# Scores and value products of a full attention as two streams over seven shared exponential buffers

## The chip, the cores and the metric

The kernel runs on one core of a Trainium2 chip. The metric is the device time of one execution in microseconds (us); lower is better. TensorE is called PE in the profile, VectorE DVE, ScalarE ACT, GpSimd POOL, and SyncE, which here only issues DMAs, SP.

## The reference

Four residual layers run in turn on x of 2048 rows by 512 columns: A, B, A, B, each behind a layer norm.

```python
# A: 32 query heads of 16, one shared key and value head
p = softmax(einsum("bhqd,bkd->bhqk", q, k) * 16 ** -0.5)        # 32 x 2048 x 2048
o = einsum("bhqk,bkd->bhqd", p, v)
x = x + o.reshape(S, 512) @ wo
# B: four segments of 512 rows, causal inside a segment, 32 heads of 16,
#    and a memory M, z that earlier segments leave behind
p = softmax(einsum(qs, ks) * 16 ** -0.5 + causal_mask)
a_mem = (phi(qs) @ M) / (phi(qs) @ z + 1e-6)
o = sigmoid(beta) * a_mem + (1 - sigmoid(beta)) * (p @ vs)
M, z = M + phi(ks).T @ vs, z + sum(phi(ks))
x = x + o @ wo
```

Everything is float32 outside; inside, projections are split into two parts each and scores into bf16 parts.

## The kernel before

**The full attention (A).** Its work is cut into units: one block `b` of 512 query rows, one group `n` of four heads, key tiles `k0` to `k1` of 128 keys. For each key tile there are two *scores*, each eight matmuls into a pair of PSUM banks (`bank<-qa,kst`, four column tiles of the array times two heads), and behind each score one *exponential* on ACT that reads the pair and writes 128 x 1024 numbers to SBUF (`pa<-bank`, line 640). Then comes one *value product* for the key tile: four float32 matmuls in the four column tiles (`bank<-pa,va`; each shows as two in the trace), which add to the one bank `pva`. The last product of a unit is followed by a transpose on DVE (line 669), and the first product of the next waits for it. There are 1024 key tiles: 2048 scores and exponentials and 1024 products.

**The windowed attention (B) and the rest.** A `side` is everything else that one block needs: the output projection of A (`out_norm`), the norm, the projections (lines 378, whole array, twelve matmuls into one bank), B's row maxima (`bank<-kb,qb`, with DVE line 838 behind them), B's scores (`bank<-qb,kb`), exponentials (`pb<-bank`, line 873) and products (`bank<-pb,vb`), the memory, and B's output projection. Projections and transposes use the whole array; scores, row maxima and products of both attentions use it as four column tiles.

**What sets the order.** The program is one stream per engine, in order. `a_units` is a Python generator that yields a time function before each step; `weave` runs it against the generator of a `side`. `weave` keeps a planned clock per engine (`clk`), asks both generators when their next step can start, adds a charge for a change of tiling (`2 * DRAIN`, 190 ns) and a small one for the one that is ahead (`LAG`), and writes the step with the lower sum. When the side is done, `finish` writes what is left of A in this phase. There are eight phases: phase 0 weaves A's first block with the preparation (norm, keys, queries), phases 1 to 7 weave one block of A with the side of the block before. After phase 7 the last side runs alone.

**Buffers.** `rings["sc"]` is the ring of PSUM pairs for scores: three pairs while A runs alone, two when A and B are woven, and then both attentions' scores take from the same ring. A pair is free again when its exponential has run. Exponentials of A rotate over four SBUF buffers (`pa`), those of B over three (`pb`). One bank (`r`) serves the projections of a woven side and one (`m`) its row maxima.

In `a_units` the order within A is fixed: score, score, then the product of the key tile before (`pend`). In `b_attend` it is: all scores of a key tile, then the product of the tile before.

Of the kernel before, what the change touches and what calls it, by code (L numbers as in the profile page):

```python
# [29 lines left out]
F32 = mybir.dt.float32  # L30
# [7 lines left out]
P = 128  # L38
# [3 lines left out]
GUARD_MAX = 160.0  # L42
KA = 5
# [28 lines left out]
def net_kernel(ctx, tc, x_in, a_wq, a_wk, a_wv, a_wo, b_wq, b_wk, b_wv, b_wo, b_beta, cst, out):  # L72
# [115 lines left out]
    xl = st([P, 4, 512], F32R, "xl")  # L188
    bank = ps_1.tile([P, 8, 512], F32, tag="bank", name="bank")
# [112 lines left out]
    class Need:  # L302


        def __init__(self, at, form):
            self.at, self.form_ = at, form
# [34 lines left out]
    def weave(za, ta, gb, tb):  # L341

        zb = [gb, next(gb)]
        da = db = 0.0
        while zb[1] is not None:
            now, ra, rb = clk["pe"], za[1]() if za[1] else 1e18, zb[1]()
            lag = (da / ta - db / tb) * (ta + tb) / 2

            def score(z, r, ahead):
                return max(now, r) + (2 * DRAIN if form_of(z[1]) != tiling[0] else 0.0) + LAG * ahead  # L350

            use = za if za[1] and score(za, ra, lag) <= score(zb, rb, -lag) else zb
# [252 lines left out]
    def a_units(units):  # L605

        def gate(f, n, k1):
            return 0.0 if f <= phase[0] or (f == phase[0] + 1 and (n == 0 or k1 < 16)) else 1e18  # L610

        def load(ui):
            L, _, b, n, _, _ = units[ui]
            return a_load(L, b, n) if L["qr"][b][n // 2] < 1e17 else None

        pend = None
        nxt = load(0)
        for ui, (L, f, b, n, k0, k1) in enumerate(units):
            if pend is not None and (gate(f, n, k1) or nxt is None):
                yield Need(lambda: max(pend[-1], pva_free[0] if pend[1] else 0.0), "cols")  # L620
                a_pv(*pend)
                pend = None
            if nxt is None:
                yield lambda: L["qr"][b][n // 2]
                nxt = load(ui)
            q, need = nxt
            if L["exact"]:
                need = yield from a_exact_guard(L, q, need)
            rows = 98 if L["exact"] else 97
            for kt in range(k0, k1):  # L630
                pe_, te = [], []
                for u in range(2):
                    yield Need(lambda: max(need, rings["sc"].ready(), L["kr"][kt // 4], gate(f, n, k1)), "cols")
                    ring = rings["sc"]
                    k, sc = ring.take()
                    for i in range(2):
                        by_columns(i == 0, sc[:, i, :], L["kst"][0:rows, kt * P:(kt + 1) * P],
                                   q[0:rows, 2 * u + i, :], start=True, stop=True)
                    x = tmp(4, [P, 2, 512], F32, "pa")
                    A.activation(x, sc, AF.Exp, scale=0.25)  # L640
                    ring.free[k] = on("act", pe(432, "cols"), 904)
                    pe_.append(x)
                    te.append(ring.free[k] + HOP)
                if kt == k0 + 1 or (kt == k0 and k1 - k0 == 1):
                    nxt = load(ui + 1) if ui + 1 < len(units) else None
                if kt == max(k0, k1 - 3) and (b, n) in L["part"]:
                    L["old"] = tmp(2, [P, 16, 32], F32, "xn")
                    nc.sync.dma_start(L["old"], L["part"].pop((b, n)))
                if pend is not None:
                    yield Need(lambda: max(pend[-1], pva_free[0] if pend[1] else 0.0), "cols")  # L650
                    a_pv(*pend)
                pend = (L, kt == k0, kt, pe_, (f, b, n, k0, k1), kt == k1 - 1, max(te))
        yield Need(lambda: max(pend[-1], pva_free[0] if pend[1] else 0.0), "cols")
        a_pv(*pend)
# [3 lines left out]
    def a_pv(L, first, kt, x, unit, last, _):  # L658
# [3 lines left out]
        for j in (2, 3, 0, 1):  # L662
            together(j == 2, pva[32 * j:32 * j + 17, :], lhsT=L["va"][:, kt, 0:17], rhs=x[j // 2][:, j % 2, :],
                     start=first, stop=last)
        e = pe(848, "cols")
        if not last:
            return
# [182 lines left out]
    def b_attend(b, n, r, last):  # L850
# [3 lines left out]
        for kt in range(4):  # L854
            nq = 512 - kt * P
            es, loc = [], ([(0, 0), (1, 0)] if kt < 2 else [(0, 0), (0, nq)])
            for s_ in range(1 if kt >= 2 else 2):
                yield Need(lambda: max(gr[n], rings["sc"].ready()), "cols")
# [13 lines left out]
                e = tmp(3, [P, 2, 512], F32, "pb")  # L872
                A.activation(e[:, :, 0:w], sc[:, :, 0:w], AF.Exp, scale=0.25)  # L873
# [40 lines left out]
    def b_pv(t, p, kt, nq, es, loc, _):  # L914
        for j in (2, 3, 0, 1):
# [3 lines left out]
                     rhs=es[s_][:, i, o_:o_ + nq], start=kt == 0, stop=kt == 3)  # L919
        pe(nq * 4 / 2.4, "cols")  # L920

# [188 lines left out]
```

## Time and profile before

| | |
|---|---|
| time, median of 3 runs | 3312.0 us (3307.43 to 3313.17) |
| the profiled execution: its time, its span | 3313.73 us, 3311.9 us |
| PE busy | 3161.7 us (95%) |
| ACT busy | 2378.2 us (72%) |
| DVE busy | 1643.2 us (50%) |
| POOL busy | 404.4 us (12%) |
| mean share of the 16 DMA engines | 18.0% for the queues of SP, 6.9% for those of POOL |
| granted TensorE clock | 0.992 of full speed |

How to read it: a matmul's row has a start and a drawn length, but matmuls are pipelined: the next group can start while the last one is still drawn. So the distance between two starts is what a group costs, and a short wait of PE can lie hidden under the drawn length. "L81" is the first matmul of a group in column tiles, "L84" the others, "L378" a projection. "Idle before" is the time in which an engine had nothing drawn, with what ended it.

### The profile page before, as it was taken

Reading aid. Unit: us, or ns where it says so; the run is one execution under the profiler, and the core shown is the slowest. Engines: PE = TensorE matmul, PEld = TensorE weight load, DVE = VectorE, ACT = ScalarE, POOL = GpSimd, SP = SyncE. Lnnn points to the kernel's source line nnn. Section 1 sums busy time; section 2 is a strip of 40 time slices with the busy share of each in tenths; the row PEclk is TensorE's granted clock in tenths of the full one; section 3 lists DMA queues with packets and bytes.
Section 4 is the critical chain, followed back from the end, with each engine's and each line's share of the span. In section 5 each row is a group of like instructions: output and inputs, shape, how many; then the busy total and the mean of one; then the engine's idle time right before and its main releaser. Section 6 shows DMA issues by size and latency. Waiting matters only on the chain.

```text
span 3311.9 us, 99350 instructions
## 1 busy us (share of the span) xinstructions
PE 3161.7 (95%) x43490; PEld 1550.1 (47%) x43490; DVE 1643.2 (50%) x4487; ACT 2378.2 (72%) x2575; POOL 404.4 (12%) x564
## 2 busy tenths in 40 slices
PE   7999999999999999999999999999999999999987
PEld 4533445444444444444444444454444444444554
DVE  7711355354654545644455453565445534454465
ACT  3599677866778667786677868677678886778533
POOL 2100111021100211101210020100110003100011
PEclk9999999999999999999999999999999999999999
DMA  4411222122220222202322142421221204421351
GB/s 132 129 42 31 61 82 61 32 76 88 68 68 17 75 77 72 66 27 65 100 84 81 45 121 84 117 65 50 87 84 47 65 25 139 126 62 41 104 147 50
DMA packets 188853, 247.56 MB, mean 75 GB/s; under 512 B 26904, under 2 KB 147576, under 8 KB 188408
## 3 DMA queue, kind: packets, MB, share of 16 engines
q1 hardware_dynamic: 169272, 176.08, 18.0%
q0 software_dynamic: 19136, 65.02, 6.9%
q8 instruction: 343, 5.62, 0.7%
q14 instruction: 102, 0.84, 0.1%
HBM read 168.41 MB, written 72.61 MB: 73 GB/s over the span
## 4 chain that ended last, share of the span: by engine, by line
PE 56%; ACT 17%; issue 11%; DVE 9%; DMA 4%; POOL 3%; SPq 0%; ACTq 0%; DVEq 0%; POOLq 0%
PE bank L81 30%; ACT pa L640 14%; PE bank L84 13%; PE bank L378 12%; ACT pb L873 3%; DMA wst<-in_B_wk_dram 2%; POOL w L134 1%; DVE w L222 1%; DVE m L813 1%; PE bank L438 1%; DVE mo L838 1%; DVE qf L456 1%; DVE rest L465 1%; POOL parts L134 1%; DVE parts L467 1%
## 5 line engine op out<-in xcount | busy, mean ns | idle before, releaser
L640 ACT ACTIVATE pa<-bank 128x1024 f32<-128x1024 f32 x2048 | 1985.2, 1030 | 536.9 <-PE bank L84 525.4
L84 PE MATMUL bank<-qa,kst 97*32 97x512 bf16 x14336 | 1175.9, 382 | 0.4 <-DVE qmx L508 0.4
L81 PE MATMUL bank<-pa,va 128*17 128x512 f32 x2048 | 1053.8, 595 | 13.3 <-DVE t L669 8.7
L84 PE MATMUL bank<-pa,va 128*17 128x512 f32 x6144 | 1063.4, 596 | 0.0
L81 PE MATMUL bank<-qa,kst 97*32 97x512 bf16 x2048 | 781.1, 381 | 40.7 <-ACT pa L640 18.0
L838 DVE CUSTOM_DVE_ANT_0 mo<-bank,maskq 128x256 bf16<-128x256 f32 (+3 forms) x896 | 436.4, 487 | 482.4 <-PE bank L84 471.6
L84 PEld LDWEIGHTS <-kst 97*32 97x32 bf16 x14336 | 360.2, 96 | 391.0 <-issue 327.1
L873 ACT ACTIVATE pb<-bank 128x1024 f32<-128x1024 f32 (+2 forms) x384 | 329.5, 881 | 179.5 <-PE bank L84 177.3
L81 PEld LDWEIGHTS <-kst 97*32 97x32 bf16 x2048 | 194.3, 95 | 379.2 <-issue 299.2
L378 PE MATMUL bank<-xh,w 128*128 128x512 f32 x832 | 292.2, 413 | 5.8 <-DVE qmx L508 3.0
L81 PEld LDWEIGHTS bank<-pa,va 128*17 128x17 f32 x2048 | 184.1, 97 | 232.5 <-ACT pa L640 51.6
L134 POOL TENSOR_SCALAR w<-wst 128x512 fp32r<-128x512 f32 x160 | 115.3, 721 | 1283.3 <-PE bank L378 1203.3
L84 PE MATMUL bank<-kb,qb 96*32 96x512 bf16 x3448 | 255.1, 296 | 0.0
L378 PE MATMUL bank<-w,xh 128*128 128x512 f32 x752 | 247.3, 409 | 6.4 <-DVE xt L712 2.5
L81 PE MATMUL bank<-kb,qb 96*32 96x512 bf16 (+2 forms) x648 | 218.0, 339 | 23.2 <-DVE m L838 12.9
L84 PE MATMUL bank<-qb,kb 98*32 98x512 bf16 (+3 forms) x3584 | 220.0, 301 | 0.0
L84 PEld LDWEIGHTS bank<-pa,va 128*17 128x17 f32 x6144 | 199.7, 98 | 0.2
L378 PEld LDWEIGHTS bank<-xh,w 128*128 128x128 f32 x832 | 158.9, 191 | 83.3 <-issue 33.5
L669 DVE STREAM_TRANSPOSE t<-bank 128x512 f32<-128x512 f32 x88 | 62.7, 713 | 265.5 <-PE bank L84 265.5
L81 PE MATMUL bank<-pb,vb 128*17 128x512 f32 (+3 forms) x512 | 180.9, 435 | 3.8 <-ACT pb L873 3.5
L84 PE MATMUL bank<-pb,vb 128*17 128x512 f32 (+3 forms) x1536 | 182.9, 435 | 0.0
L222 DVE TENSOR_TENSOR w<-wst,w 128x512 fp32r<-128x512 f32 x160 | 112.6, 704 | 129.5 <-POOL w L134 128.9
(153 smaller groups left out, 3368.8 us busy)
## 6 DMA issues: line engine op xcount, KB each, us to landing
sb<-parts SPq DMA_DIRECT2D x192, 128.0 KB
qa<-sd SPq DMA_DIRECT2D x88, 196.0 KB
sd<-parts SPq DMA_DIRECT2D x96, 128.0 KB
x<-xt SPq DMA_DIRECT2D x48, 256.0 KB
xt<-x SPq DMA_DIRECT2D x48, 256.0 KB
qb<-sb SPq DMA_DIRECT2D x64, 192.0 KB
kb<-sb SPq DMA_DIRECT2D x64, 192.0 KB
qa<-sd SPq DMA_DIRECT2D x88, 128.0 KB
```

The source lines that it names most:

```text
L81: nc.tensor.matmul(*a, **k)
L84: tc.keep_in_program_order(nc.tensor.matmul(*a, **k))
L134: G.tensor_scalar(o, i, 1.0, 0.0, op0=ALU.mult, op1=ALU.add)
L222: V.tensor_tensor(w[:, 1, :], s, f(w[:, 0, :]), op=ALU.subtract)
L378: T.matmul(ps, lhsT=l_(kt), rhs=r_(kt), start=n == 0, stop=n == 11)
L438: T.transpose(ps[:, k, :], xn[:, k * P:(k + 1) * P], ident)
L456: V.tensor_copy(x, ps)
L465: V.tensor_tensor(r, x, parts[:, 0, :], op=ALU.subtract)
L640: A.activation(x, sc, AF.Exp, scale=0.25)
L669: V.transpose(t1.rearrange("p a b -> p (a b)"), pva)
L838: V.tensor_tensor_reduce(out=mo[:, 0:nk], in0=ps[:, o_:o_ + nk], in1=maskq[:, 512 - nk:512], op0=ALU.add, op1=ALU.max, scale=1.0, scalar=- ...
L873: A.activation(e[:, :, 0:w], sc[:, :, 0:w], AF.Exp, scale=0.25)
```

## The change

A's scores and products become two streams. The scores are a generator `scores()`; each finished key tile is put into a `queue`, and `product()` tells when the first of the queue can run. The outer loop of `a_units` writes a score if one can start no later than now or than the first product, else a product. `Need` gets a third entry, `put_off`, which `weave` adds to A's sum: -1000 (`FEED`) when a score could start, +1000 (`DEFER`) when only a product could, +2000 when it is the only one in the queue. Both attentions take their exponentials' buffers from one list of seven (`ebuf`; `e_take`, `e_give`, `e_has`), the same memory as four and three; a score of A needs two free ones when products are queued (`E_LEFT`), else one. `b_attend` writes the product of the tile before behind the first score of a tile, no longer behind its last. The load of an earlier partial result (`L["old"]`) moves from the scores to the products.

```diff
+DEFER = 1000.0
+FEED = -1000.0
+E_LEFT = 1
...
+    ebuf = [st([P, 2, 512], F32, f"e{i}") for i in range(7)]
+    e_free, e_at = list(range(len(ebuf))), [0.0] * len(ebuf)
+
+    def e_take():
+        i = min(e_free, key=lambda z: e_at[z])
+        e_free.remove(i)
+        return i
+
+    def e_give(i):
+        e_free.append(i)
+        e_at[i] = clk["pe"]
+
+    def e_has(n):
+        return 0.0 if len(e_free) >= n else 1e18
...
-            use = za if za[1] and score(za, ra, lag) <= score(zb, rb, -lag) else zb
+            use = za if za[1] and score(za, ra, lag) + za[1].put_off() <= score(zb, rb, -lag) else zb
...
-                    x = tmp(4, [P, 2, 512], F32, "pa")
-                    A.activation(x, sc, AF.Exp, scale=0.25)
...
-                if pend is not None:
-                    yield Need(lambda: max(pend[-1], pva_free[0] if pend[1] else 0.0), "cols")
-                    a_pv(*pend)
-                pend = (L, kt == k0, kt, pe_, (f, b, n, k0, k1), kt == k1 - 1, max(te))
...
+        queue = []
+        def scores():
...
+                    for u in range(2):
+                        yield lambda: max(need, rings["sc"].ready(), L["kr"][kt // 4], gate(f, n, k1),
+                                          e_has(E_LEFT + 1 if queue else 1))
...
+                        x = e_take()
+                        A.activation(ebuf[x], sc, AF.Exp, scale=0.25)
...
+                    queue.append((L, kt == k0, kt, es, (f, b, n, k0, k1), kt == k1 - 1, max(te)))
+
+        def product():
+            return max(queue[0][-1], pva_free[0] if queue[0][1] else 0.0) if queue else 1e18
+
+        def put_off():
+
+            if z is not None and z() <= max(clk["pe"], product()):
+                return FEED
+            return 2 * DEFER if len(queue) == 1 else DEFER
+
+        g = scores()
+        z = next(g)
+        while z is not None or queue:
+            yield Need(lambda: min(z() if z is not None else 1e18, product()), "cols", put_off)
+            zs, zp = z() if z is not None else 1e18, product()
+            if zs <= max(clk["pe"], zp):
+                z = next(g, None)
+            else:
+                a_pv(*queue.pop(0))
...
+        for i in x:
+            e_give(i)
+        if kt == max(k0, k1 - 3) and (b, n) in L["part"]:
+            L["old"] = tmp(2, [P, 16, 32], F32, "xn")
+            nc.sync.dma_start(L["old"], L["part"].pop((b, n)))
...
-                yield Need(lambda: max(gr[n], rings["sc"].ready()), "cols")
+                yield Need(lambda: max(gr[n], rings["sc"].ready(), e_has(1)), "cols")
...
-            if pend is not None:
-                yield Need(lambda: max(pend[4], v_r[0], pvb_free[0] if pend[0] == 0 else 0.0), "cols")
-                b_pv(t, p, *pend)
+                if pend is not None:
+                    yield Need(lambda: max(pend[4], v_r[0], pvb_free[0] if pend[0] == 0 else 0.0), "cols")
+                    b_pv(t, p, *pend)
+                    pend = None
```

Lines 81 and 84 of the program before are lines 84 and 87 of the changed one, line 378 is 397, and an exponential's tile is called `e` instead of `pa` or `pb`.

**On PE, at the value projections of a woven side** (`bank<-xh,w` is a projection, `bank<-qa,kst` a score of A, the row with `va` its product; each row that stands for a group is its first, the rest of the group is left out). Before:

```order
L81 MATMUL bank<-pa_11320,va_16_106 17x512
...
L81 MATMUL bank<-qa_18_112,kst_14_104 32x512
...
L378 MATMUL bank<-xh_139,w_11064 128x512
L378 MATMUL bank<-xl_140,w_11064 128x512
...
L81 MATMUL bank<-qa_18_112,kst_14_104 32x512
...
L81 MATMUL bank<-pa_11362,va_16_106 17x512
```

and with the change:

```order
L84 MATMUL bank<-e_39_141,va_16_106 17x512
...
L397 MATMUL bank<-xh_139,w_10417 128x512
L397 MATMUL bank<-xl_140,w_10417 128x512
...
L84 MATMUL bank<-qa_18_112,kst_14_104 32x512
...
L84 MATMUL bank<-qa_18_112,kst_14_104 32x512
...
L397 MATMUL bank<-xh_139,w_10417 128x512
L397 MATMUL bank<-xl_140,w_10417 128x512
...
L84 MATMUL bank<-e_45_147,va_16_106 17x512
```

The twelve matmuls of one projection stood together; now two scores stand in the middle of them, and the product that stood between two scores has gone behind the projection.

**On PE, beside the row maxima of B** (`bank<-kb,qb`). Before:

```order
L81 MATMUL bank<-pa_12085,va_16_106 17x512
...
L81 MATMUL bank<-qa_19_113,kst_14_104 32x512
...
L81 MATMUL bank<-kb_24_118,qb_21_115 32x512
...
L81 MATMUL bank<-qa_19_113,kst_14_104 32x512
...
L81 MATMUL bank<-pa_12109,va_16_106 17x512
```

and with the change:

```order
L84 MATMUL bank<-e_45_147,va_16_106 17x512
...
L84 MATMUL bank<-qa_19_113,kst_14_104 32x512
...
L84 MATMUL bank<-qa_19_113,kst_14_104 32x512
...
L84 MATMUL bank<-kb_24_118,qb_21_115 32x384
...
L84 MATMUL bank<-e_41_143,va_16_106 17x512
```

Row maximum and product stood between single scores; now both scores of a key tile stand together, then the row maximum, then one product, over and over.

More of the change, by code (lines that the diff above doesn't have):

```diff
@@ L302, in net_kernel, with __init__ @@
     class Need:
-        def __init__(self, at, form):
-            self.at, self.form_ = at, form
+        def __init__(self, at, form, put_off=lambda: 0.0):
+            self.at, self.form_, self.put_off = at, form, put_off
         def __call__(self):
@@ L614, in load @@
             return a_load(L, b, n) if L["qr"][b][n // 2] < 1e17 else None
[L616 to L619, printed above, removed]
-                yield Need(lambda: max(pend[-1], pva_free[0] if pend[1] else 0.0), "cols")
-                a_pv(*pend)
[L622 to L638, printed above, removed]
-                    x = tmp(4, [P, 2, 512], F32, "pa")
[L640 to L648, printed above, removed]
-                if pend is not None:
-                    yield Need(lambda: max(pend[-1], pva_free[0] if pend[1] else 0.0), "cols")
-                    a_pv(*pend)
-                pend = (L, kt == k0, kt, pe_, (f, b, n, k0, k1), kt == k1 - 1, max(te))
@@ L653, in a_units @@
-        yield Need(lambda: max(pend[-1], pva_free[0] if pend[1] else 0.0), "cols")
-        a_pv(*pend)
+        queue = []
+        def scores():
+            nxt = load(0)
+            for ui, (L, f, b, n, k0, k1) in enumerate(units):
+                if nxt is None:
+                    yield lambda: L["qr"][b][n // 2]
+                    nxt = load(ui)
+                q, need = nxt
+                if L["exact"]:
+                    need = yield from a_exact_guard(L, q, need)
+                rows = 98 if L["exact"] else 97
+                for kt in range(k0, k1):
+                    es, te = [], []
+                    for u in range(2):
+                        yield lambda: max(need, rings["sc"].ready(), L["kr"][kt // 4], gate(f, n, k1),
+                                          e_has(E_LEFT + 1 if queue else 1))
+                        ring = rings["sc"]
+                        k, sc = ring.take()
+                        for i in range(2):
+                            by_columns(i == 0, sc[:, i, :], L["kst"][0:rows, kt * P:(kt + 1) * P],
+                                       q[0:rows, 2 * u + i, :], start=True, stop=True)
+                        x = e_take()
+                        A.activation(ebuf[x], sc, AF.Exp, scale=0.25)
+                        ring.free[k] = on("act", pe(432, "cols"), 904)
+                        es.append(x)
+                        te.append(ring.free[k] + HOP)
+                    if kt == k0 + 1 or (kt == k0 and k1 - k0 == 1):
+                        nxt = load(ui + 1) if ui + 1 < len(units) else None
+                    queue.append((L, kt == k0, kt, es, (f, b, n, k0, k1), kt == k1 - 1, max(te)))
@@ L662, in a_pv @@
         for j in (2, 3, 0, 1):
-            together(j == 2, pva[32 * j:32 * j + 17, :], lhsT=L["va"][:, kt, 0:17], rhs=x[j // 2][:, j % 2, :],
+            together(j == 2, pva[32 * j:32 * j + 17, :], lhsT=L["va"][:, kt, 0:17], rhs=ebuf[x[j // 2]][:, j % 2, :],
                      start=first, stop=last)
         e = pe(848, "cols")
+        for i in x:
[3 more added lines that the diff above has]
+            nc.sync.dma_start(L["old"], L["part"].pop((b, n)))
         if not last:
@@ L871, in b_attend @@
                 w = loc[1][1] + nq
-                e = tmp(3, [P, 2, 512], F32, "pb")
-                A.activation(e[:, :, 0:w], sc[:, :, 0:w], AF.Exp, scale=0.25)
+                e = e_take()
+                A.activation(ebuf[e][:, :, 0:w], sc[:, :, 0:w], AF.Exp, scale=0.25)
                 es.append(e)
@@ L918, in b_pv @@
             together(j == 2, pvb[32 * j:32 * j + 17, kt * P:512], lhsT=vb[:, kt, 8 * t + 2 * j + p, :],
-                     rhs=es[s_][:, i, o_:o_ + nq], start=kt == 0, stop=kt == 3)
+                     rhs=ebuf[es[s_]][:, i, o_:o_ + nq], start=kt == 0, stop=kt == 3)
         pe(nq * 4 / 2.4, "cols")
+        for i in es:
+            e_give(i)
     def b_memory(b, t, r):
```

## The prediction

> **What bounds the kernel now.** I read the page's head first, then the busy time by stage, then PE's groups with the idle time before them, then short stretches of the timeline.
>
> ```profile
> PE 3161.7 (95%) x43490; PEld 1550.1 (47%) x43490; DVE 1643.2 (50%) x4487; ACT 2378.2 (72%) x2575; POOL 404.4 (12%) x564
> ```
>
> PE is nearly full over the whole span and ACT is not. By stage (engine busy times, then granted clock, DMA share and GB/s):
>
> ```profile
> core 0: us, PE busy (x) PEld busy (x) DVE busy (x) ACT busy (x) POOL busy (x), PEclk, DMA share, GB/s
> 0.00:162.00 162.00, 138.53 (x1076) 77.64 (x1080) 121.03 (x271) 76.91 (x92) 35.60 (x56) 0.98 0.46 131
> 162.00:353.00 191.00, 189.39 (x2481) 64.25 (x2473) 25.24 (x51) 189.69 (x207) 4.13 (x7) 1.00 0.13 36
> 353.00:1983.00 1630.00, 1578.07 (x21639) 773.83 (x21633) 829.71 (x2322) 1199.21 (x1289) 207.74 (x276) 1.00 0.24 69
> 1983.00:2046.00 63.00, 61.55 (x805) 22.12 (x799) 23.03 (x48) 61.51 (x68) 2.47 (x4) 1.00 0.31 88
> 2046.00:3110.00 1064.00, 1026.12 (x14821) 504.05 (x14818) 520.80 (x1526) 797.80 (x856) 124.04 (x174) 1.00 0.25 73
> 3110.00:3311.90 201.90, 168.01 (x2690) 108.21 (x2690) 123.36 (x270) 53.06 (x69) 30.41 (x48) 0.94 0.39 120
> ```
>
> The second and fourth rows are A alone: ACT is busy 189.69 of 191 us, so there the exponentials are the bound. The third and fifth are the woven stages, 2694 us together: ACT is busy 74%, PE 97%, and PE stands visibly for only 51.9 + 37.9 = 90 us. The last row is the side that runs alone. The change can act on the woven stages above all. What PE waits for there, in a view of its groups from 353 to 3110 us (busy, mean ns, idle just before and its releasers):
>
> ```profile
> L81 PE MATMUL bank<-pa,va 128*17 128x512 f32 x1782 | 916.8, 595 | 12.1 <-DVE t L669 8.4 <-DVE y L425 3.3
> L81 PE MATMUL bank<-qa,kst 97*32 97x512 bf16 x1781 | 679.3, 381 | 38.7 <-ACT pa L640 16.8 <-ACT pb L873 11.7
> L81 PE MATMUL bank<-pb,vb 128*17 128x384 f32 x112 | 45.5, 487 | 3.4 <-ACT pb L873 3.2
> ```
>
> Products of A wait for 12.1 us, mostly for the transpose between units; scores for 38.7 us, for the exponential that still holds their PSUM pair. The drawn lengths hide more. A place beside row maxima, where the program of before happens to have the pattern that the changed one has throughout (score, score, row maximum, product):
>
> ```profile
> 3036.45 0.38 PE L81 MATMUL bank<-qa,kst 97*32 97x512 bf16 x1
> 3037.21 0.38 PE L81 MATMUL bank<-qa,kst 97*32 97x512 bf16 x1
> 3037.64 0.27 PE L81 MATMUL bank<-kb,qb 96*32 96x256 bf16 x1
> 3037.86 0.59 PE L81 MATMUL bank<-pa,va 128*17 128x512 f32 x1
> ...
> 3038.72 0.38 PE L81 MATMUL bank<-qa,kst 97*32 97x512 bf16 x1
> 3039.16 0.38 PE L81 MATMUL bank<-qa,kst 97*32 97x512 bf16 x1
> ...
> 3040.67 0.38 PE L81 MATMUL bank<-qa,kst 97*32 97x512 bf16 x1
> 3041.44 0.38 PE L81 MATMUL bank<-qa,kst 97*32 97x512 bf16 x1
> ```
>
> A score takes 0.43 us (3037.21 to 3037.64), a row maximum 0.22, a product 0.86 (to 3038.72). But from 3036.45 to 3037.21 and from 3040.67 to 3041.44 it is 0.76: 0.33 us are lost before the second score, no idle time is shown, and it happens in every other round. A round is thus about 1.95 + 0.17 us. Two PSUM pairs and an exponential of about 0.9 us make this, whatever the product does.
>
> **The change part by part.** I count along the order of instructions of both programs; the prices are rows.
>
> *Products.* In the order before, 848 of 1024 products stand right behind a score, in the changed one 415; 351 stand behind a step of B (148 before), 213 behind a projection or transpose (28), 45 behind another product (0). Their exponentials are then older, and the scores of the next unit stand in front of a unit's first product, so its wait for the transpose is covered by them. I take off the whole row: -12 us. Bounds: 0, if the waits move to the next instruction, and -20 with as much again hidden as two thirds of it.
>
> *Scores.* A pair is taken by every second score. In the woven stages, 434 scores have under 1.75 us of PE work between the taking before last and themselves; in the changed order 289, a third less. I let a third of the 38.7 us go, 13, and as much of what is hidden, because the place above loses 0.33 us twice with nothing shown: -26 us. Bounds: -40 (all of the shown row), and +10, because the pattern that loses 0.33 in every other round stands for about 200 key tiles now, where single scores stood between other steps before, and 60 more such losses of 0.17 would be 10.
>
> *Changes of tiling.* They go from 692 to 826, 67 more pairs, mostly because 98 projections instead of 28 have scores put into their middle. Their price:
>
> ```profile
> 404.13 0.39 PE L378 MATMUL bank<-xl,w 128*128 128x512 f32 x1
> 404.35 0.40 PE L378 MATMUL bank<-xh,w 128*128 128x512 f32 x1
> 404.68 0.39 PE L81 MATMUL bank<-qa,kst 97*32 97x512 bf16 x1
> ...
> 407.29 0.59 PE L81 MATMUL bank<-pa,va 128*17 128x512 f32 x1
> ...
> 407.83 0.50 PE L378 MATMUL bank<-xh,w 128*128 128x512 f32 x1
> 408.16 0.39 PE L378 MATMUL bank<-xl,w 128*128 128x512 f32 x1
> 408.39 0.40 PE L378 MATMUL bank<-xh,w 128*128 128x512 f32 x1
> ```
>
> Inside a projection a matmul follows after 0.22 or 0.23 us; the last before a score takes 0.33 (0.10 more), half a product before a projection 0.54 instead of half of 0.86 (0.11 more), the first of a projection 0.33 (0.10 more). A pair of changes costs 0.31 us: 67 x 0.31 = +21 us. It is PE's own time, so nothing hides it. Bounds: +7 with 0.11 a pair, +21.
>
> *Projections closer together.* With one bank, a projection must wait until the one before is read out:
>
> ```profile
> 3113.67 0.40 PE L378 MATMUL bank<-w,xl 128*128 128x512 f32 x1
> 3114.11 0.69 DVE L712 TENSOR_TENSOR xt<-xt,bank 128x512 f32<-128x512 f32 x1
> 3114.85 0.73 PE L378 MATMUL bank<-w,xh 128*128 128x512 f32 x2 [0.78 <-DVE xt L712]
> ```
>
> The last matmul's 0.23 us end at 3113.90, and the next can start 0.95 later. In the changed order 34 such pairs have only 0.72 to 0.87 us of other work between them, none had under 1.0 before: 34 x 0.1 = +3 us (0 to +8).
>
> *B's products.* Putting the product of a key tile behind the first score of the next one brings the 384-wide product nearer to its exponential in 27 of 56 places. The row shows 3.4 us of waits for 56 of them; I double it: +3 us (0 to +15, at 0.5 us for each of 27). The shared buffers add no wait of their own: B always finds one free, since A's scores leave it one.
>
> *A alone.* Long runs of A without a step of another kind hold 137 products before and 175 now, and there the exponentials set the pace. Three rounds of the second stage:
>
> ```profile
> 199.51 0.60 PE L81 MATMUL bank<-pa,va 128*17 128x512 f32 x1
> ...
> 201.34 0.60 PE L81 MATMUL bank<-pa,va 128*17 128x512 f32 x1
> ...
> 203.17 0.60 PE L81 MATMUL bank<-pa,va 128*17 128x512 f32 x1
> ```
>
> 1.83 us a key tile, against 2 x 0.43 + 0.86 = 1.73 of PE work: 38 x 0.1 = +4 us (0 to +6).
>
> *The end.* Of the projections behind the last product of A, 45 matmuls (nearly four projections) now stand before it. The row at 3114.85 shows what each of those four loses when it runs alone, 0.78 us; B's side has then ended with A: -4 us (0 to -8).
>
> *Costs nothing:* the later load of 24 partial results, two key tiles (3.7 us) ahead of the addition on DVE that reads it, and DVE is half idle; SP's queue keeps its order around it. If it lands late, DVE waits, and PE only at the next unit's first product.
>
> Sum: -12 - 26 + 21 + 3 + 3 + 4 - 4 = -11 us. The profiled execution took 3313.7 us, 1.7 more than the median of the runs, so 3303 for it and **3301 us** for the median. 0.2%, 6.6 us, is about what a measurement of this kernel can tell from no change.
>
> Here a rule speaks against the purpose of the change. At one place PE stood for long although other work was near:
>
> ```profile
> 562.55 0.59 PE L81 MATMUL bank<-pa,va 128*17 128x512 f32 x1
> ...
> 564.05 0.38 PE L81 MATMUL bank<-qa,kst 97*32 97x512 bf16 x1 [0.90 <-ACT pa L640]
> ...
> 564.48 0.38 PE L81 MATMUL bank<-kb,qb 96*32 96x512 bf16 x1
> ```
>
> with, on ACT before it,
>
> ```profile
> 562.46 0.63 ACT L765 ACTIVATE phk<-phk 128x512 f32<-128x512 f32 x1 [1.03 <-DVE phk L764]
> ```
>
> ACT stood 1.03 us for DVE, the exponential behind came late, PE stood 0.90 us, and the row maximum of 564.48 did not pass the score. Such waits are not in the plan, and a kept product cannot take their place unless it was written there. The Trainium skill says so in general (TensorE: Matmul & The Clock Gate, section "Step-by-step: what each phase is for"): "The MATMULs themselves stay in program order". The trace agrees with it at this place; were it otherwise, the first rival's 60 us would be the forecast.
>
> **The rivals.**
>
> *Much faster.* The kept products fill most of PE's visible idle time in the woven stages. Two thirds of the 90 us would be -60: 3252 us. For it: idle time is there and products have no one waiting for them except buffers. Against it: the place at 564.05, and the products of the changed order stand mostly one key tile behind, as before. Chance 0.15.
>
> *Slower.* `FEED` and `DEFER` make the plan prefer a score that is ready only before the product is, and a step of B that will be ready within 1 us, though a product could go now; and the plan's clock does not move on by that wait. On the chip PE stands there. Its price is the 0.33 us of the row at 3037.21. From 11 / 0.33 = 33 such stands more than I count the gain is gone, from (11 + 6.6) / 0.33 = 53 the kernel is measurably slower. If the 200 rounds with the new pattern lose 0.33 us each, not every other one, that is 200 x 0.165 = +33 us and the sum -11 + 33 = +22: 3334 us. For it: the pattern in the row above, and 134 changes of tiling more. Chance 0.33.
>
> *No change.* A score still waits for a pair of two, and waits only move: within 6.6 us of 3312. For it: 930 scores of the woven stages have under 2 us of PE work behind the taking before last, 937 before. Chance 0.22.
>
> **How the numbers follow.** The small gain (3270 to 3305) has 0.30, much faster 0.15, no change 0.22, slower 0.33. Faster by over 0.2% is 0.30 + 0.15 = 0.45. The range from 3245 to 3345 reaches past the rivals' 3252 and 3334 and leaves out 2 in 10; the likeliest case's own bounds are the sums of the ends: 3312 - 20 - 40 + 7 - 8 = 3251 and 3312 + 0 + 10 + 21 + 8 + 15 + 6 = 3372, with all at one end unlikely.
>
> **What would show it.** Right: idle time before `e,va` products near zero; before scores about 25 us from 353 us to the last product; PE busy about 10 us higher in the woven stages by the changes of tiling; the last stage some 10 us shorter. Wrong: products still wait, or row maxima and projections have taken over the waits that scores lost (idle before `bank<-kb,qb` or L397 grown by over 15 us); or scores behind a score lose 0.33 us in every round. A time under 3270 would mean that waits out of the plan were filled after all.

## The result, and the profile after

The changed kernel takes 3361.06 us (median, 3356.37 to 3367.82) against 3312.59 us before: ratio 1.015, 95% interval 1.0129 to 1.0172. It is 1.5% slower, and lies 16 us above the range of the prediction. The profiled execution has a span of 3366.0 us, 54.1 more than before; of the four executions it was the longest, 6.8 us above the median, so not all of the 54 us are in the difference of the medians, 48.5.

The engines' busy times on the page after:

```profile
PE 3194.3 (95%) x43490; PEld 1558.8 (46%) x43490; DVE 1639.8 (49%) x4487; ACT 2374.8 (71%) x2575; POOL 404.5 (12%) x564
```

The work is the same, instruction for instruction, but PE's busy time has grown by 32.6 us and its idle time by 21.5. The same six stages as shown of before, cut where they now begin and end (columns as there):

```profile
0.00:162.00 162.00, 137.20 (x1072) 77.05 (x1072) 121.74 (x274) 76.60 (x92) 37.23 (x58) 0.99 0.45 129
162.00:358.00 196.00, 191.90 (x2478) 73.70 (x2474) 24.08 (x49) 189.75 (x208) 2.48 (x4) 0.98 0.12 36
358.00:2004.00 1646.00, 1580.60 (x21491) 767.21 (x21495) 823.57 (x2320) 1187.04 (x1277) 207.16 (x276) 1.00 0.23 67
2004.00:2079.00 75.00, 74.01 (x971) 30.35 (x964) 24.10 (x50) 73.63 (x81) 2.52 (x5) 1.00 0.29 87
2079.00:3175.00 1096.00, 1053.02 (x14856) 510.69 (x14854) 528.19 (x1535) 794.85 (x854) 126.93 (x178) 0.99 0.25 73
3175.00:3366.00 191.00, 157.54 (x2638) 99.82 (x2634) 118.15 (x262) 52.92 (x68) 28.17 (x45) 0.92 0.38 116
```

The woven stages (third and fifth row) take 2742 us, 48 more than before: 29 of it is PE busy, 19 idle. The stages of A alone take 17 more, the last stage 11 less: 48 + 17 - 11 = 54. What PE waits for in the woven part, by groups from 358 to 3175 us (busy, mean ns, idle just before and its releasers):

```profile
L84 PE MATMUL bank<-e,va 128*17 128x512 f32 x1784 | 911.9, 596 | 5.8 <-DVE t L703 5.7
...
L84 PE MATMUL bank<-qa,kst 97*32 97x512 bf16 x1781 | 677.8, 381 | 41.7 <-ACT e L658 28.9 <-ACT e L907 0.8
...
L397 PE MATMUL bank<-w,xh 128*128 128x512 f32 x672 | 228.1, 420 | 15.0 <-DVE xl L465 14.0 <-DVE xt L746 0.4 <-DVE t L928 0.2
...
L84 PE MATMUL bank<-e,vb 128*17 128x384 f32 x112 | 45.6, 488 | 6.6 <-ACT e L907 6.2
```

Products wait 5.8 us, half of the 12.1 before. Scores, which were to wait less, wait 41.7 instead of 38.7. B's 384-wide products wait 6.6 instead of 3.4. B's products of all widths and the row maxima, over the whole run before

```profile
L81 PE MATMUL bank<-pb,vb 128*17 128x512 f32 (+3 forms) x512 | 180.9, 435 | 3.8 <-ACT pb L873 3.5
...
L81 PE MATMUL bank<-kb,qb 96*32 96x512 bf16 (+2 forms) x648 | 218.0, 339 | 23.2 <-DVE m L838 12.9
```

and with the change:

```profile
L84 PE MATMUL bank<-e,vb 128*17 128x512 f32 (+3 forms) x512 | 181.1, 435 | 13.0 <-ACT e L907 12.1
...
L84 PE MATMUL bank<-kb,qb 96*32 96x512 bf16 (+2 forms) x648 | 219.4, 341 | 31.0 <-DVE m L872 17.6
```

Projections now have 14.0 us of waits for one DVE operation (`xl`, line 465), in six stands of PE; one of them, in the timeline:

```profile
380.91 0.38 PE L84 MATMUL bank<-qa,kst 97*32 97x512 bf16 x1
...
381.35 0.38 PE L84 MATMUL bank<-qa,kst 97*32 97x512 bf16 x1
...
382.73 0.69 DVE L241 TENSOR_TENSOR w<-wst,w 128x512 fp32r<-128x512 f32 x1 [1.45 <-POOL w L137]
383.33 0.68 DVE L463 CAST xh<-bank 128x512 fp32r<-128x512 f32 x1
...
384.05 0.69 DVE L465 TENSOR_TENSOR xl<-bank,xh 128x512 fp32r<-128x512 f32 x1
...
384.80 0.73 PE L397 MATMUL bank<-w,xh 128*128 128x512 f32 x2 [2.84 <-DVE xl L465]
```

The second score ends at 381.78 (0.43 us behind its start) and the projection starts at 384.80: PE stands for 3.0 us. On DVE the operands of the projection stand in the queue behind `w`, which waits 1.45 us for POOL. No step of A was written between. At the other five stands `w` waits for POOL too, 0.7 to 1.4 us.

The growth of the busy time has two parts. Most of it goes with the changes of tiling: with 696 of them instead of 826 (e5 below) PE is busy for 22.7 us less,

```profile
PE 3171.6 (95%) x43490; PEld 1564.2 (47%) x43490; DVE 1640.4 (49%) x4487; ACT 2368.3 (71%) x2575; POOL 398.1 (12%) x564
```

although it keeps the pattern that follows. The rest, some 10 us, is the growth of waits that the drawn lengths hide. The first matmuls of the groups in two rounds beside row maxima, from the timeline:

```profile
864.87 0.38 PE L84 MATMUL bank<-qa,kst 97*32 97x512 bf16 x1
...
865.31 0.38 PE L84 MATMUL bank<-qa,kst 97*32 97x512 bf16 x1
...
865.74 0.38 PE L84 MATMUL bank<-kb,qb 96*32 96x512 bf16 x1
...
865.96 0.59 PE L84 MATMUL bank<-e,va 128*17 128x512 f32 x1
...
866.82 0.38 PE L84 MATMUL bank<-qa,kst 97*32 97x512 bf16 x1
...
867.59 0.38 PE L84 MATMUL bank<-qa,kst 97*32 97x512 bf16 x1
...
869.10 0.38 PE L84 MATMUL bank<-qa,kst 97*32 97x512 bf16 x1
```

Score, score, row maximum, product, over and over. The round from 864.87 takes 1.95 us, the one from 866.82 takes 2.28: its second score starts 0.77 behind the first instead of 0.44, since the exponential still holds its pair. No idle time is drawn. This is the place at 3037.21 of the kernel before, which had 11 such rounds (score, score, row maximum, product, and two scores again); the changed one has 172. They last 2.146 us on average, and the second scores lose 28.9 us in sum, 0.168 a round: 0.2 to 0.5 in most of some 84, 0.33 above all, and next to nothing in nearly all the others. The Trainium skill (Perfetto Trace Analysis, section "Identifying the Most-Contended Engine") calls the busy share of matmuls a poor measure of how near a kernel is to its limit, because pipelined matmuls look smaller in the trace. This trace agrees that it is a poor measure, with 32.6 us more of it for the same matmuls.

Those 28.9 us are not what scores lose more than before, since scores at other places lose less. An account of all starts of PE shows it: the distance from each group to the next one, less what such a group costs without a wait (0.43 us a score, 0.86 a product, 0.22 a row maximum, 0.23 a matmul of a projection, 0.31 a pair of changes of tiling). What is left is a wait, shown or hidden, and is put down to the group that starts late. It is an estimate; other choices of these prices, but for that of a change of tiling, move a difference by about 1 us. In the profiled executions, in us:

| | forecast | before | with the change | difference |
|---|---|---|---|---|
| changes of tiling, woven part | +21 | 90 | 111 | +21 |
| waits before A's scores, woven part | -26 | 102 | 103 | 0 |
| of these, second scores of the rounds above | | 2.5 | 28.8 | +26 |
| before A's products, woven part | -12 | 17 | 12 | -5 |
| before projections and the transposes for their operands, woven part | +3 | 12 | 27 | +15 |
| before B's products, woven part | +3 | 7 | 22 | +15 |
| before row maxima, woven part | none | 26 | 32 | +6 |
| before B's scores, woven part | none | 22 | 19 | -3 |
| all waits, stages of A alone | +4 | 18 | 24 | +6 |
| all waits and changes, first and last stage | -4 | 77 | 78 | +1 |

The differences add up to 56; what is left of the account is 2 us shorter, which gives the 54 us of the two spans.

### The profile page after: what moved, and what is told of

It is laid out like the page before. It is cut to its first block, busy times and chain, and to the rows that moved or that the text cites. A ratio compares the mean times of both kernels' runs of the same rounds, so it can differ in the third digit from the quotient of the medians.

```text
span 3366.0 us, 100360 instructions
## 1 busy us (share of the span) xinstructions
PE 3194.3 (95%) x43490; PEld 1558.8 (46%) x43490; DVE 1639.8 (49%) x4487; ACT 2374.8 (71%) x2575; POOL 404.5 (12%) x564
## 4 chain that ended last, share of the span: by engine, by line
PE 56%; issue 15%; ACT 14%; DVE 8%; DMA 4%; POOL 2%; SPq 0%; ACTq 0%; DVEq 0%; POOLq 0%
PE bank L84 29%; PE bank L397 13%; PE bank L87 13%; ACT e L658 12%; ACT e L907 2%; POOL w L137 1%; DMA wst<-in_B_wk_dram 1%; DVE m L847 1%; PE bank L457 1%; DVE mo L872 1%; DVE w L241 1%; DVE parts L486 1%; DMA sb<-parts 1%; DVE rest L484 1%; DVE qf L475 1%
## 5 line engine op out<-in xcount | busy, mean ns | idle before, releaser
L658 ACT ACTIVATE e<-bank 128x1024 f32<-128x1024 f32 x2048 | 1978.5, 1080 | 582.8 <-PE bank L87 573.7
L87 PE MATMUL bank<-qa,kst 97*32 97x512 bf16 x14336 | 1157.2, 381 | 0.1
L87 PE MATMUL bank<-e,va 128*17 128x512 f32 x6144 | 1059.5, 597 | 0.0
L84 PE MATMUL bank<-e,va 128*17 128x512 f32 x2048 | 1048.3, 596 | 9.5 <-DVE t L703 9.4
L84 PE MATMUL bank<-qa,kst 97*32 97x512 bf16 x2048 | 779.5, 381 | 44.8 <-ACT e L658 31.3
L87 PEld LDWEIGHTS <-kst 97*32 97x32 bf16 x14336 | 380.5, 96 | 457.4 <-issue 392.3
L907 ACT ACTIVATE e<-bank 128x1024 f32<-128x1024 f32 (+2 forms) x384 | 329.4, 880 | 139.2 <-PE bank L87 135.8
L84 PEld LDWEIGHTS <-kst 97*32 97x32 bf16 x2048 | 194.5, 95 | 402.5 <-issue 312.6
L397 PE MATMUL bank<-xh,w 128*128 128x512 f32 x832 | 300.5, 417 | 7.0 <-DVE qmx L527 3.4
L84 PEld LDWEIGHTS bank<-e,va 128*17 128x17 f32 x2048 | 172.9, 97 | 205.9 <-issue 84.6
L84 PE MATMUL bank<-e,vb 128*17 128x512 f32 (+3 forms) x512 | 181.1, 435 | 13.0 <-ACT e L907 12.1
L87 PEld LDWEIGHTS bank<-e,va 128*17 128x17 f32 x6144 | 189.9, 97 | 0.8
L87 PE MATMUL bank<-e,vb 128*17 128x512 f32 (+3 forms) x1536 | 183.5, 435 | 0.0
L397 PEld LDWEIGHTS bank<-w,xh 128*128 128x128 f32 x752 | 134.2, 191 | 100.2 <-issue 28.9
```

Of the source, the lines that this page charges most:

```text
L84: nc.tensor.matmul(*a, **k)
L87: tc.keep_in_program_order(nc.tensor.matmul(*a, **k))
L397: T.matmul(ps, lhsT=l_(kt), rhs=r_(kt), start=n == 0, stop=n == 11)
L658: A.activation(ebuf[x], sc, AF.Exp, scale=0.25)
L907: A.activation(ebuf[e][:, :, 0:w], sc[:, :, 0:w], AF.Exp, scale=0.25)
```

## The experiments

All ratios are to the kernel before, which had a median of 3310.7 to 3313.1 us beside them. The changes of tiling are counted in each program (692 before, 826 in the changed kernel).

| run | what differs from the changed kernel | us | ratio, 95% interval | changes of tiling |
|---|---|---|---|---|
| e1 | no put-off at all | 3299.97 | 0.9963 (0.9949 to 0.9977) | 724 |
| e2 | `FEED` 0 | 3322.12 | 1.0036 (1.0021 to 1.0051) | 788 |
| e3 | `DEFER` 0 | 3347.30 | 1.0112 (1.0095 to 1.0129) | 842 |
| e4 | plan's clock follows the chosen step | 3346.34 | 1.0112 (1.0096 to 1.0129) | 794 |
| e5 | projections in one piece | 3338.86 | 1.0080 (1.0063 to 1.0096) | 696 |
| e6 | score preferred only if ready now | 3329.06 | 1.0056 (1.0038 to 1.0074) | 848 |
| e7 | e1, and B's product where it was | 3292.74 | 0.9938 (0.9921 to 0.9954) | 714 |
| e8 | (kernel before, B's product moved alone) | 3299.85 | 0.9968 (0.9953 to 0.9982) | not counted |
| e9 | e2 and e5 | 3339.87 | 1.0086 (1.0069 to 1.0103) | 700 |
| e10 | e3, e5, e6, and B's product where it was | 3284.45 | 0.9911 (0.9895 to 0.9928) | 670 |
| e11 | e7 and e5 | 3291.84 | 0.9938 (0.9921 to 0.9954) | 716 |
| e12 | e7 and e4 | 3296.81 | 0.9949 (0.9932 to 0.9966) | 710 |
| e13 | e5 and e6 | 3317.41 | 1.0016 (1.0006 to 1.0025) | 690 |
| e14 | e3, e5 and e6 | 3290.41 | 0.9938 (0.9921 to 0.9954) | 694 |
| e15 | e13, held only if B's step is ready | 3313.91 | 1.0003 (0.9994 to 1.0012) | 700 |
| e16 | held only if B's step is ready | 3359.79 | 1.0141 (1.0126 to 1.0157) | 786 |
| e17 | e15, and ready for 1 us or more | 3303.56 | 0.9975 (0.9966 to 0.9983) | 700 |
| e18 | e15, and ready for less than 1 us | 3292.60 | 0.9936 (0.9921 to 0.9951) | 690 |

**Which part costs the time.** The put-off, its two halves, and the other parts without it.

```diff
-DEFER = 1000.0
-FEED = -1000.0
+DEFER = 0.0      # e1, e3, e7
+FEED = 0.0       # e1, e2, e7
```

> FEED and DEFER are both 0; two streams, the seven shared buffers and the new place of B's products stay. Theory K (the put-off rule makes PE stand in front of steps that are not ready while a product could go): the loss is gone, 3300 to 3322 us. Theory S (the loss is the price of the changes of tiling): they are 724 instead of 826 here, 32 more than before the change, at 0.16 us each +5, so 3317 us; S and K do not differ here. Theory B (shared buffers and the place of B's products cost it): 3345 us or more.

> Only FEED is 0: a score is no longer drawn ahead, products are still held back. 788 changes of tiling. K with the holding back as its main part: 3340 to 3361 us; K with the drawing ahead of scores as its main part: 3312 to 3335 us. S: 96 changes more than before, +15, 3327 us. B: 3345 us or more.

> Only DEFER is 0: products are not held back, scores are still drawn ahead. 842 changes of tiling. K with the holding back as its main part: 3312 to 3340 us, above all less idle time before projections; K with the drawing ahead as its main part: 3340 to 3361 us. S: 150 changes more than before, +24, 3336 us, and more than with FEED at 0. B: 3345 us or more.

e7 is e1 with B's product written behind the last score of a tile again, and e8 is the kernel before with only that product moved:

```diff
-            if pend is not None:
-                yield Need(...)
-                b_pv(t, p, *pend)
+                if pend is not None:      # inside the loop over a tile's scores
+                    yield Need(...)
+                    b_pv(t, p, *pend)
+                    pend = None
```

> Two streams and seven shared buffers with FEED and DEFER at 0, and B's products where they stood before the change. If the gain of the run without put-off (0.9963) comes from the streams and the buffers: 3295 to 3305 us. If it comes from the new place of B's products: 3306 to 3316 us.

> The kernel before with one edit: B's product stands behind the first score of the next key tile. If the gain of the run without put-off comes from here: 3295 to 3305 us; if not: 3306 to 3318 us.

The put-off carries the whole loss: without it (e1) the kernel is 61 us faster than the changed one and 0.4% faster than before. Taking away `FEED` gives 39 of the 61 back, taking away `DEFER` 14; the other 8 come back only when both go. So each costs more where the other is missing: `FEED` 47 us (e3 against e1), `DEFER` 22 (e2 against e1). The two streams with the shared buffers gain 0.6% (e7), and B's product gains 0.3% in the old order (e8). These gains don't add: with the streams it loses 7 us (e1 against e7; the two intervals overlap). The rows agree: idle time before B's products is 9.0 us in e1 and 0.7 in e7.

**The score that goes before its pair is free.** e6 prefers a score only if it can start at the plan's present time, e4 lets the plan's clock move on by the wait of the step that it chose.

```diff
-            if z is not None and z() <= max(clk["pe"], product()):
+            if z is not None and z() <= clk["pe"]:            # e6
...
-            clk["pe"] = t0 = max(now, min(ra, rb))
+            clk["pe"] = t0 = max(now, ra if use is za else rb)   # e4
```

> The changed kernel, but FEED is given only when a score can start now, not when it can start before the first product. 848 changes of tiling, 22 more than the changed kernel. K with scores drawn ahead before they are ready: 3315 to 3335 us, near the run with FEED at 0 (3322). S: 3361 us or above. If what costs is that a score goes ahead of B at all, ready or not: 3345 to 3361 us.

> As the changed kernel, but the plan's clock moves to the time at which the chosen step can start, not to the earlier of the two. 794 changes of tiling. If the harm comes through a plan that no longer knows where PE stands (part of K): 3315 to 3340 us. If the plan is right and the choice itself costs: 3350 to 3365 us. S: 102 changes more than before, +16, 3328 us.

e6 gives 32.0 us back, though it changes the tiling more often (848). Its page's busy times, the group of A's scores over the whole run (44.8 us of idle before it in the changed kernel), and two rounds beside row maxima from its timeline:

```profile
PE 3175.3 (95%) x43490; PEld 1552.7 (47%) x43490; DVE 1629.0 (49%) x4487; ACT 2378.1 (71%) x2575; POOL 397.5 (12%) x564
```

```profile
L84 PE MATMUL bank<-qa,kst 97*32 97x512 bf16 x2048 | 780.2, 381 | 24.5 <-ACT e L658 21.3
```

```profile
854.60 0.38 PE L84 MATMUL bank<-qa,kst 97*32 97x512 bf16 x1
...
855.03 0.38 PE L84 MATMUL bank<-kb,qb 96*32 96x512 bf16 x1
...
855.36 0.38 PE L84 MATMUL bank<-qa,kst 97*32 97x512 bf16 x1
...
855.79 0.59 PE L84 MATMUL bank<-e,va 128*17 128x512 f32 x1
...
856.65 0.38 PE L84 MATMUL bank<-qa,kst 97*32 97x512 bf16 x1
...
858.61 0.38 PE L84 MATMUL bank<-qa,kst 97*32 97x512 bf16 x1
```

The row maximum now stands between the two scores. The rounds take 2.05 and 1.96 us, where the changed kernel needs 1.95 and 2.28. The old pattern is left in 10 rounds and loses 1.1 us there; idle time before scores is 20 us less and PE's busy time 19 us less, and with the same matmuls and more changes of tiling that can only be hidden waits. So the condition of `FEED` costs 32 us. This isn't what the scores lose against the kernel before: by the account above, over the whole run, waits before A's scores are 110 us before, 126 with the change and 81 in e6, where B's scores pay 16 of it back. Nor are the rounds all that `FEED` costs: with `FEED` 0 (e2) 39 us come back, though 114 of the rounds are left and lose 20.9 us; there the waits before projections are 15 us less and those before scores 16. The clock alone (e4) gives 15 us back; 142 of the rounds are left and lose 19.9 us.

**Projections in pieces.** `project` offers a place between its halves, where a score that `FEED` prefers can go in.

```diff
-            if kt == 1:
-                yield lambda: 0.0
```

> The changed kernel, but a projection's twelve matmuls are written without the pause in their middle, so no score can go between. 696 changes of tiling, as many as before the change (692); FEED and DEFER stay. Theory S (changes of tiling, at about 0.16 us each by the rows of before, or more): 3361 less 130 x 0.16 = 3340 us or below. Theory K (PE stands for steps written before they are ready): 3340 to 3361 us, and scores behind scores go on losing.

22.2 us come back for 130 fewer changes: 0.17 us a change, 0.34 a pair, against 0.31 from the rows of before. The Trainium skill (TensorEngine Tiling (Array Packing), section "Key Properties") says that a change of tiling mode drains the TensorE, without a figure; the rows agree: over the traces of all versions a score in front of a projection takes 0.11 us more, a projection's first matmul 0.11 and its last 0.10 (medians). But e5 moves other things too. By the account the profiled executions differ by 20 us of changes, 17 less before projections (the idle time for `xl` falls from 14.0 to 1.4 us) and 9 less before row maxima, and by 15 more before scores: their idle time grows from 44.8 to 56.4 us, and 183 of the bad rounds lose 31.2. So the 0.17 us a change is partly a balance of these, and e16, which has 40 changes fewer but another order, gains only 1.3 us.

**Put together.**

> FEED 0, DEFER 1000, projections written whole: 700 changes of tiling, against 788 with FEED 0 alone (3322 us). If what holding back costs is the changes of tiling that it makes: 88 x 0.16 = 14 less, 3308 us, near the run without put-off (3300). If holding back costs through PE standing in front of row maxima and projections: 3315 to 3325 us, with idle time before row maxima as with FEED 0 alone.

> Streams alone (B's products as before the change, DEFER 0), FEED -1000 given only when a score can start now, projections whole: 670 changes of tiling, against 714 in the streams alone (3293 us). If drawing ahead a score that is ready helps (idle time before scores falls as in the run that fed when ready, 24.5 us) and changes of tiling cost 0.16 each: 3293 - 7 - 10 = 3276 us. If a score that is drawn ahead takes from B what it gives A: 3286 to 3300 us.

> Streams alone with projections whole: 716 changes of tiling, two more than the streams alone (3293 us), since scores seldom went into a projection there. S: 3288 to 3298 us. If the pause in a projection serves something else (a bank free sooner, a score in time): 3300 us or more.

> Streams alone with the plan's clock moved to the time at which the chosen step can start: 710 changes of tiling. Without FEED and DEFER the plan seldom chooses a step that is not ready, so the clock should matter little: 3286 to 3298 us. If the clock's error by itself makes the order worse: under 3286 us.

> The changed kernel with both edits that each gave something back: FEED only when a score can start now (32 us), projections whole (22 us); DEFER stays at 1000. 690 changes of tiling. If the two causes are apart and are the whole loss: 3361 - 32 - 22 = 3307 us. If holding products back costs by itself: 3318 us or more; long runs of A alone hold 240 products here, 175 in the changed kernel, which at 0.1 us would be 7 of it.

> The run above with DEFER 0: 694 changes of tiling, 151 products in long runs of A. What lies between the two is the price of holding back by itself. If there is none: within 6 us of the run above. If it is what the two edits leave: 3285 to 3300 us, since the kernel without put-off took 3300.

With e5's and e6's edits together (e13) 44 us come back, of 54 if they added. Without `DEFER` another 27 follow (e14). So the 71 us from 3361 to 3290 are: 32 by the condition of `FEED`, 22 by projections in one piece, 27 by holding products back, less 10 where they overlap. e10, which also leaves B's product in its old place, is the fastest version: 0.9% faster than before, and between its two expectations. In it FEED still works, with a score that is ready. Without any put-off, whole projections (e11) and the true clock (e12) bring nothing. e9 stays open in part: with `FEED` 0, whole projections made it 18 us slower than e2, although it has 88 fewer changes of tiling; the row of its products shows 15.2 us of waits for the transpose, 7.5 in e2, and that of its scores 47.2 us of idle time, 38.3 in e2.

**What holding back costs.** Groups before which PE waits for DVE, over the whole run, in e13 (with `DEFER`):

```profile
L397 PE MATMUL bank<-xh,w 128*128 128x512 f32 x832 | 293.6, 415 | 14.1 <-DVE qf L473 7.1 <-DVE qmx L525 3.0 <-DVE w L241 1.3
...
L455 PE MATMUL bank<-cs,xn 128*128 128x128 f32 x256 | 43.1, 295 | 16.5 <-DMA wst<-in_A_wk_dram 11.8 <-DVE xl L463 2.8 <-DVE xt L744 1.5
...
L807 PE MATMUL bank<-cs,phk 128*128 128x128 f32 x96 | 16.0, 290 | 13.7 <-DVE phk L798 13.7
```

and in e14 (without):

```profile
L397 PE MATMUL bank<-xh,w 128*128 128x512 f32 x832 | 293.1, 415 | 5.2 <-DVE qmx L525 2.3 <-DVE t L926 0.9 <-DVE w L271 0.8
...
L455 PE MATMUL bank<-cs,xn 128*128 128x128 f32 x256 | 43.7, 298 | 12.3 <-DMA wst<-in_A_wk_dram 12.1 <-DVE xn L452 0.2
...
L807 PE MATMUL bank<-cs,phk 128*128 128x128 f32 x96 | 15.6, 285 | 0.0
```

Two explanations offered themselves: PE stands before steps of B that the plan prefers though they aren't ready (`phk`), or A runs alone for longer, 445 us in eight stretches (of more than 15 us without another step) in e13 against 251 in two in e14. e15 and e16 take the first away:

```diff
-            use = za if za[1] and score(za, ra, lag) + za[1].put_off() <= score(zb, rb, -lag) else zb
+            put = za[1].put_off() if za[1] else 0.0
+            put = min(put, 0.0) if rb > now else put
+            use = za if za[1] and score(za, ra, lag) + put <= score(zb, rb, -lag) else zb
```

> The version with scores sent only when ready and whole projections (3317), and now a product is held back only if the step of B can start at once; the preference for scores stays. 700 changes of tiling against 690 there. Theory A (holding back costs because the plan takes a step of B that becomes ready up to 1 us later, while a product could go, and PE stands before that step): most of the 27 us come back, 3290 to 3298, and the idle time before L807 (phk), 13.7 us there, falls under 3. Theory B (the holding itself costs: products bunch, B's side is done sooner and A runs alone for longer): 3310 to 3320, the stretches of A alone stay about 460 us.

> The changed kernel with one edit: a product is held back only if the step of B can start at once. 786 changes of tiling against 826. Theory A (waits before steps of B that are not ready): 14 us as without any holding back, so 3340 to 3348. Theory B: only the 40 fewer changes count, 0.17 us each, 3352 to 3358.

Both fall. In e15 `phk` waits 3.6 us and A runs alone for 249 us, as in e14, and yet only 3.5 of the 27 us are back; in e16 1.3 of 14. The waits have moved, in e15, to

```profile
L399 PE MATMUL bank<-xh,w 128*128 128x512 f32 x832 | 294.5, 415 | 17.4 <-DVE qf L475 10.5 <-DVE qmx L527 2.2 <-DVE t L928 1.8
...
L457 PE MATMUL bank<-cs,xn 128*128 128x128 f32 x256 | 43.3, 297 | 27.5 <-DVE xl L465 15.0 <-DMA wst<-in_A_wk_dram 12.1 <-DVE xn L454 0.4
```

which suggested a third: B's steps are written the moment that the plan takes them for ready, and DVE is later. e17 and e18 split the held products by that:

```diff
-            put = min(put, 0.0) if rb > now else put
+            put = min(put, 0.0) if rb > now - 1000.0 else put             # e17
+            put = put if now - 1000.0 < rb <= now else min(put, 0.0)      # e18
```

> e15 with one number changed: a product is held back only if the step of B has been ready for 1 us or more in the plan. Holding back then turns the choice 375 times, 804 times in e15. Theory C (holding back takes the slack: B's step is written as soon as the plan takes it for ready, DVE is later on the chip, and PE stands): most of the 24 us between e15 and the version without holding come back, 3290 to 3297, and the idle time before L457 and L399 falls from 57 to under 35 us. Rival D (each product held back costs, whatever the slack): in proportion to the count, 3301.

> The opposite of e17: a product is held back only if the step of B has become ready within the last 1 us of the plan; 291 choices turned. Theory C: the loss stays, 3308 to 3316, and the idle time before L457 and L399 stays at 50 us or more. Rival D: in proportion to the count, 3299.

The third falls too, with the opposite sign: holding back for a step that has only just become ready costs nothing that can be told (2 us against e14), for one that has been ready for 1 us or more 13. The idle time before L457 and L399 is 39.5 us in e17 and 35.8 in e18, where theory C had under 35 and over 50. Nor is it the mere number: 804 choices turned cost 23.5 us, 375 cost 13, 291 cost 2; rival D's number is met for e17 and missed by 6 us for e18. That holding back costs 27 us is shown, and so are three things that don't explain it; which of the held products does it stays open.

## Why the prediction was wrong

**The scores' term failed: -26, where the waits before scores did not fall.** In the woven part their shown waits grew by 3 us (38.7 to 41.7), and with the hidden ones they are 102 us before and 103 with the change. The scores outside the new pattern did lose less, as forecast: 100 us before, 74 with the change. The rounds of score, score, row maximum, product put the same 26 us back. The step behind it was a threshold. I counted scores with under 1.75 us of PE work since the taking before last, found a third fewer, and let waits go in proportion. But in the round score, score, row maximum, product that work is 1.95 us, above the threshold for both scores, and my own row at 3037.21 showed that such a round still loses 0.33 every other time. I had the price (0.17 a round) and the number of rounds ("about 200"), and their product, some 30 us, stood only in a bound, as 60 losses and +10.

**The slower rival had the mechanism.** It named `FEED`'s condition, and the clock that doesn't move on. Its price came out by a wrong step: it took 0.33 in every round; measured are 0.168, about every other round, as in the row. Its 33 us stood on top of the -26, and so it ended at 3334; that they are near the 32 which e6 gives back is chance, since e6 takes the scores' waits far below those of the kernel before. What it said of `DEFER`, that PE stands before a step of B ready within 1 us, is a small part of what holding back costs (e15).

**What else the sum lacked.** With 0 for the scores' -26 the sum is +15, and +48.5 was measured. Most of the rest are waits in front of steps of B's side: before projections +15 instead of +3, before B's products +15 instead of +3, before row maxima +6 where the sum had nothing. The sum's terms for B's side were the bank and one width of product, and that is where it was short by some 30 us. The runs show that the put-off as a whole costs 61 us (e1); how its price divides over these rows is read from the account of one execution each and not shown by an experiment of its own. B's products wait in e1 too, so their part goes at least partly with their new place.

**The other terms.**
- *Products*, -12: 12.1 to 5.8 us in the woven part, and 17 to 12 with the hidden waits. Half of it. With the put-off off, 1.7 us are left of 13.3 in the whole run (e1). Why the put-off brings them back was not followed.
- *Changes of tiling*, +21: the price of the rows holds in all traces, and the changes came as counted. Right.
- *Projections closer*, +3: the wait for the bank is not what grew. The 14.0 us are DVE's `xl`, late behind `w` in DVE's queue, a wait that the prediction didn't have. The transposes for the operands wait 7 us less, so +15 in all.
- *B's products*, +3: the 384-wide ones went from 3.4 to 6.6 us, as forecast, but all widths from 3.8 to 13.0, and with the hidden waits by +15. Too small by 12.
- *A alone*, +4: stretches without another step went from 255 to 309 us, some 29 key tiles at 1.83 us instead of 1.73, 3 us; the account has +6. About right.
- *The end*, -4: the last stage is 10.9 us shorter (201.9 to 191.0), but some 10 us of that are projections that moved into the woven part (45 matmuls at 0.23). Waits before its projections fell by 5 us, as forecast, and others grew: the first and last stage together gained nothing.

**The fast rival** expected 60 us from PE's idle time. The row at 564.05 spoke against it, and the stand behind 381.35 is the same: no step of A had been written there, and the wait was not filled. The best version found (e10) gains 28.6 us. 21 of them are there without any put-off (e11); preferring a score only if it is ready adds 7.

## What to carry to other kernels

A planner that may put a step ahead of others must ask whether it is ready now, not whether it will be ready before its rival: in a program that each engine runs in order, a preferred step that waits holds everything behind it (32 us here). Two uses of the same small ring of buffers were better separated by other work than put side by side (2.0 us a round in e6 against 2.1 in the rounds shown), and whether a pattern waits is read from the distance between starts in the trace, in every round of it, not from a threshold on the work between. When a pattern is in the trace of before at one place and the change repeats it 170 times, price by count is the term, not the bound. And what one edit gives back is not what the change had cost at that place: an account by starts, over all groups and both programs, tells the two apart.

## What the runs showed of the hardware

With two PSUM pairs, four column tiles and exponentials drawn 1.08 us long on average, the wait before a second score came in about every other round, 0.33 and 0.01 us in turn where rounds followed one another, and PE's drawn busy time took it up. A change between the whole array and column tiles costs some 0.3 us for going and coming back (0.11 before a projection, 0.11 at its first matmul, 0.10 at its last), and it counts as busy too. So PE's busy time was itself a sign of both: 3194.3 us in the changed kernel, 3175.3 in e6 with more changes of tiling, 3171.6 in e5 with more waits before scores, and

```profile
PE 3148.8 (96%) x43490; PEld 1572.0 (48%) x43490; DVE 1635.9 (50%) x4487; ACT 2378.5 (72%) x2575; POOL 401.1 (12%) x564
```

in e10, the fastest, for the same 43490 matmuls.
